# Two kinds of transposes moved from DMA to TensorE, and an in-place sum, in a fused backward kernel on one core

## The chip, the cores and the metric

The kernel runs on one NeuronCore of a Trainium2 chip. The core has a matrix engine (TensorE; PE in the profile, with its weight loads as PEld), a vector engine (VectorE, DVE), a scalar engine (ScalarE, ACT), a small general engine (GpSimd, POOL), a queue engine that here only issues DMAs (SyncE, SP), and sixteen DMA engines that all queues share. The metric is the time of one launch on the device in microseconds.

## The reference

A forward pass and its gradient are computed in one launch. In short:

```
xn  = layernorm(x)                               # 2048 x 512
K   = Re sum_n C * exp(dt*A*l) * dt*B            # 512 kernels of length 2048, 128 states each
s   = causal_conv(xn, K) + xn * Dskip            # through FFTs
f   = silu(xn @ w1) @ w2                         # 512 -> 1792 -> 512
out = x + s * silu(f)
gradients of sum(out * grad_out) for x, A, B, C (re, im), log_dt, Dskip, w1, w2
```

All inputs and outputs are bf16.

## The kernel before

The rows are held as 128 partitions x 16 tiles x 512 columns. The state-space part works by blocks b of 128 channels (4 of them), each in two halves h. The program is a set of generators, each with a letter; `play` walks through the string PLAN and lets the generator of each letter issue its next few instructions. So PLAN is an order written out by hand or by a planner, and it fixes the order of the instructions in each engine's own queue. WAYS says for each letter which of its evacuations of PSUM go to ScalarE (A) and which to DVE (D), SLOTS which buffer each tile takes. PLAN has seven parts:

- 0: loads, layer norm (6), tables (4, 5), masks (3), first rows of the forward network.
- 1: phases and powers of the state-space kernel (P, Q), its rows (R), the forward conv (X, C), the forward network (F: `gen_ffn_fwd`).
- 2: the gate (G), ds = grad_out * gate (H), transposed weights (W), forward transform of ds (D).
- 3: the backward conv (B: `gen_conv_bwd`, which leaves the gradient du in `k.ds`), dA through the network (A: `gen_da`), dx (x: `gen_dx`), the first output (O).
- 4 and 5: the gradients of A, B, C and dt. For each block, N (`gen_ssm_fold`) folds dK into G; for each of 16 groups of eight channel rows, Y (`gen_ssm_loads`) loads a transposed tile YT of the powers from DRAM, V (`gen_ssm_v`) multiplies YT with Gb into ps_v and evacuates it to Vb, T (`gen_ssm_products`) makes four products and two sums Tp, and S (`gen_ssm_sums`) sums Tp over the 21 exponents on TensorE into psS, which ScalarE copies to Sa. Z (`gen_ssm_grads`) makes the gradients of a block and stores them (gout). In part 5 also dW2 (h loads an activation block h_in, t makes a_tok = silu of it with tokens on the partitions, w multiplies) and dW1 (g loads dh_tok by DMA transposes, v multiplies).
- 6: the rest of dW1 and dW2 and the layer norm's backward: i (`gen_ln_loads`) loads pd_l (the stored dx) and Gt (grad_out), k (`gen_ln_sums`) adds du and makes two sums a row, m (`gen_ln_rows`) makes and stores the rows.

The places that the change touches:

- `gen_dw2_loads` and `gen_dw2_turns`: of 14 blocks the first nine come by a plain DMA, are turned by 16 TensorE transposes into PSUM and go through silu from there (L1197); the last five come by a DMA transpose (L1180) and go through silu in one instruction (L1194).
- `gen_ssm_loads`: every YT is two DMA transposes (L970) on SyncE's queue.
- `gen_dx`: each of 16 tiles ps_dx is evacuated to pd_s and stored to DRAM (Pd, L1171); part 6 loads it back and adds it to `k.ds` (L1270).
- `gen_ssm_fold`: ScalarE spreads G over four lanes into one tile Gf (L956); `gen_ssm_v` multiplies Gf by the masks MK into Gb (L986), both halves of Gb.
- `gen_ssm_sums`: two exponents a matmul (L1034), so psS and Sa hold two halves, which `gen_ssm_grads` adds (L1059).
- `gen_kernel_rows`: block 3's eight loads of Kb (L675) alternate between SyncE's and GpSimd's queues.

Tile pools are stacked: the last stage's pool `lw` takes the memory of `sb`, the pool of parts 4 and 5, so its first tiles wait for the last users of what lay there.

Of the kernel before, what the change touches and what calls it, by code (L numbers as in the profile page):

```python
# [10 lines left out]
ACT = mybir.ActivationFunctionType  # L11
ALU = mybir.AluOpType
# [6 lines left out]
P = 128  # L19
# [8 lines left out]
122p13273555417652067776357p577511777p747701636770773677J0J767p5787777367F66766767077F78676777633FF736746687F46F8F7486FF  # L28
F8F6666FF6F688FF56F64FJ8/XFXQFJFFFXXXPJXPXFXPFFFPXPXFPFPFQJFFFQQF9QQQFFFXFQFJQQXXQPFQXRPFFRXPXRRXFXPPFRFXPJFRRXFRPXFRQQQ
RPXQFQRQFXFRQQFFRFUFFXFQXFFFFRQRXRPRFRQXRRJPRRUPFPXRRURFRPRURQRXRFJRQCRPQFXXXXFFRQXXXQFQFQQXPQRPPFCRCCCFFFRCRCQRPCRQFRFC  # L30
RFFRFFPQRQCUQFRCFFFFCQQRFFCCQQCFCQFCXRCQQCFQCRPXFFCRXCFXCFXFPXCRPFXFCXRFCXRFJCFRRCXRPCXCFRFFQQCFRFCQQFCFRQPFFCRQPRRFCPQC
QFXFRQQRPQRCXRRRCXXJPRXRRXCUPXPRXXRCRFCPCCRQQPFFCFCFFCCPQCQFFQCRRQQCQRRXFQFCXFRFFCFQFCFCFCCCCPQJRRXCXRCCFCFFXPRRCXFPCRXC
CFCXQQCQFFQJRXPQFRCCQXCCCRQFRFQFCPRQCQRRRRRQRRRXRFPCFXRPFRFCXRCXPFURRRCXCFFRRXCCFFQFQJQQCXFXCFFCCRQCFFRCCRQQCQRFQCFRCRRR
RRCCCCXRQCCCCRCJRCRCRURRFCRRFCRCCRFFCCCCRC/CGCFCCGCCGFGFFFCCFCGCCGFGCCFGGCFCFFCGCGFCCGFCFWGCGGGGCGCFCHFCFGCGHFCCFCFCCGCH
FCGCWWCFCCCGGCWCWCCCWWHCCWCDHWHHGCCWDGMCCCWHCWWDWWDWDWLDGDWWDWWWWLWDMDDDMDDDLDDMLLWM/DEWDadDodDEDdDsBDADAAAoBDaDADdaAAAo
AsDBAoBABDWDWABADBBAasBoAAAoBBBAAAAlOBBADOaABoAADlOBBBsBxBoBDoBBDBBDEABABxDOABABxOABBBBAsxBODBoxDBxdOOBloDBoDOBxBaxDBBBD
ODEOxOBoDxBsdABBOxAOoBBBBBaAADdBDoBBaBsBBBABBBoOADAdDDAAADBAAlBoBDAAEAOooBaADBBBAddADBDABAlDBOADDADBDBAxADsoBDEOBlOAxBDO
DBAoBxxDBOABADBAABDBBADAOoABxsxDBOBoOBABAoxOABBBoOBBBADOOoDBAOoxoaBDaxDBADAdDxoBBDADBEDxOsDBBBABxAABxBOBdAOOAoBABABBBOsx
aABOBBxBsaEABxBxAABxBAABBABaBOABBdBBBxBBBaBABBBAABABBBAABABBBdBAxBsBBBsB/YNxYdYxNANNAdANAAAAxYVVAAVAVVAVaVAAxVxAVYsATAAY
NVATVxTVVAVATAVxVTVAAxsxTAVSxTAYASAVVVVAAxATAVVAVYxVTATYTTTVTxTTVxTVxVxVNTxVVSNNS/NVTVSVhTVTVVVSYTgVVtVTVhTtSSVttTVTwYTT  # L40
VTwttNhTVtgVwVSVZVVYVVthZZwtVVTNTVtTwTYZtNtwTVVTYNwZtSShvVYwtSwNVVTVVZTVTTZVVYTZtVTtVVvgVTVwTZVTZVTTtVTZSVvSVVVvSSvVVYtV
VNVVvTTvZTTVTthTZYwvVVgYtVVZZVSSTTvTVZZtwtNNwYVNthNwtTTvTVVTwVVTSVZYSVTVTwTVwVTVVvTVTTSVVYSVthVTTVZTYZTvTgStVTgZtSVVZvtv
VTVTTYVVZYVvZVhvZwSZVgtTVZtwgTvVwVVgTTgTTZvSVtwvtVvVSZVVTSTVZTVvVVZZTVwVTTTSThTwZTtSvTZZTvtSZtvwSvtZtZwvZwZvZZvZhZvwvZvZ
ZvZ/vikkgviktvwkkikigwmkhvvgvwmvigkkmvvkmvkmvihvvvwtkvmkvmvvkmikkhkvmwmkvmikwkmwvvvkwmkmvktkvvvtkmmwvkvmkwkvwkmkmkmkwwmv
wvwmmvmv
# [4 lines left out]
fp.XT=01010101;pf.pf=012012012010212120120102102102102102102102102102020210210210102102102021021021020210210210210210202  # L50
102102102102102120120210210210210210210210102102012010120120121021021021021021021021021012212012012102102012010210210210
210210202102102;fp.hT=0101010101010101;fp.ob=0101010;dft.w8=21031230132102302103210302310321;pc.pc=010101010101110101010
101010101010101010101011010101010101010101010101010101010101010101010010110101010101010101010101010110101010101010101010
101010101010101010101010101010101010101010101010101010101010101010110101010101011010101010101010101010101010101010101;tb
l.tv=01011101010110100010110100011010;tbl.ts=01010101110111010101001000101010;tbl.W=01010101010010100101;dft.t4=01001010
1010;gate.g=30124567;gate.S=01;da.doT=01010101;dftb.w8b=1010;da.dhT8=01201201;go.go_s=01010101;da.dhT6=10101010;go.go_r=
010101;go.go_g=01010101;da.pd_s=0101010101010101;go.go_x=01201201;sb.YT=0101010101010101;sb.Eb=10101010;sb.Gb=01010101;s
b.Vb=0101010101010101;sb.Tp=1010101010101010;sb.Sa=0101;fw.h_in=01010101010101;fw.a_tok=01010101010101;fw.o11=0120120120
1201;fw.dh_tok=0120120;fw.o10=0101010;lw.pd_l=01230123;lw.Gt=01230123;lw.m=01010101;lw.o1=12301230
# [100 lines left out]
def setup_tiles(k, wp):  # L160
# [28 lines left out]
    new("m4", [4])  # L189
# [22 lines left out]
def gen_plain_consts(k, w):  # L212
# [7 lines left out]
    G.memset(k.pi[:], PI_LO)  # L220
# [66 lines left out]
def gen_step_tables(k, w):  # L287
# [6 lines left out]
    pt, ph, pe, sh, kf, kk, maskf, kq, sf, sv, pj, pa, m4, rl = (  # L294
        getattr(w, nm) for nm in "p_t p_h p_e sh kf kk maskf kq sf sv pj pa m4 rl".split())
# [32 lines left out]
    TT(out=m4[:], in0=pa[:], in1=w.ia[:], op=ALU.is_equal)  # L328
    TT(out=rl[:], in0=k.ecst[:, 0:NE], in1=pj[:].to_broadcast([P, NE]), op=ALU.add)
    yield  # L330
    nc.vector.tensor_copy(out=k.MK[:, 0], in_=m4[:].unsqueeze(1).to_broadcast([P, NE, 4]))
    TT(out=k.MK[:, 1], in0=rl[:].unsqueeze(2).to_broadcast([P, NE, 4]), in1=m4[:].unsqueeze(1).to_broadcast([P, NE, 4]), op=ALU.mult)
# [290 lines left out]
def gen_kernel_rows(k, b):  # L623
# [277 lines left out]
def gen_conv_bwd(k):  # L901
# [3 lines left out]
    for b in range(4):  # L905
# [23 lines left out]
def gen_ssm_fold(k, b, sb):  # L929
# [17 lines left out]
    Gf = sb.tile([P, 32, NE, 4], BF16, name="Gf", tag="Gf")  # L947
    k.Gf[b] = Gf
# [6 lines left out]
    for bank, n in ((0, 16), (1, 5)):  # L955
        nc.scalar.copy(out=Gf[:, :, 16 * bank:16 * bank + n, :],  # L956
                       in_=G21[:, bank, 0:32 * n].rearrange("p (e q) -> p q e", e=n).unsqueeze(3).to_broadcast([P, 32, n, 4]))
        yield
# [486 lines left out]
```

## Time and profile before

| | |
|---|---|
| median of 3 runs (lowest, highest) | 576.56 us (576.12, 577.17) |
| the profiled execution | 581.0 us |
| its span, first to last instruction | 578.5 us |
| mean granted TensorE clock | 0.981 |
| PE, DVE, ACT busy | 520.2, 518.0, 451.3 us |
| HBM read, written | 58.72, 59.90 MB |

The page gives for each engine the time it was busy; the slices cut the span in forty parts and give the busy share in tenths. The view of waits lists, for each engine and line, what ended its idle time. A number of a queue (SPq, POOLq) is time in which DMAs were being issued. The window view sums busy time in a stretch. The rows of groups by line give busy us, mean ns of one, and the idle time just before them.

### The profile page before, as it was taken

Reading aid. Unit: us, or ns where it says so; the run is one execution under the profiler, and the core shown is the slowest. Engines: PE = TensorE matmul, PEld = TensorE weight load, DVE = VectorE, ACT = ScalarE, POOL = GpSimd, SP = SyncE. Lnnn points to the kernel's source line nnn. Section 1 sums busy time; section 2 is a strip of 40 time slices with the busy share of each in tenths; the row PEclk is TensorE's granted clock in tenths of the full one; section 3 lists DMA queues with packets and bytes.
Section 4 is the critical chain, followed back from the end, with each engine's and each line's share of the span. In section 5 each row is a group of like instructions: output and inputs, shape, how many; then the busy total and the mean of one; then the engine's idle time right before and its main releaser. Section 6 shows DMA issues by size and latency. Waiting matters only on the chain. (4 is left out here: it accounts for less than half of the span.)

```text
span 578.5 us, 13917 instructions
## 1 busy us (share of the span) xinstructions
PE 520.2 (90%) x5681; PEld 385.6 (67%) x5704; DVE 518.0 (90%) x814; ACT 451.3 (78%) x560; POOL 78.3 (14%) x168
## 2 busy tenths in 40 slices
PE   1497999998998989999999999999799979999983
PEld 1365768676777766876677766777567858776752
DVE  8989999999999768999999889778899989983984
ACT  7999999999998749999899866754578766643553
POOL 4321101011102030000000000000002202123221
PEclk9889999999999999999999999999899999999998
DMA  8977798988898996788779899979999999999991
GB/s 242 330 300 229 233 231 310 302 226 252 329 263 250 342 295 268 239 270 247 255 261 300 245 307 287 238 180 244 234 231 234 214 208 213 230 222 245 215 284 74
DMA packets 174032, 145.75 MB, mean 252 GB/s; under 512 B 102224, under 2 KB 151632, under 8 KB 170896
## 3 DMA queue, kind: packets, MB, share of 16 engines
q1 hardware_dynamic: 164656, 122.05, 79.0%
q0 software_dynamic: 6768, 19.93, 9.6%
q10 hardware_dynamic: 2544, 2.88, 1.5%
q8 instruction: 44, 0.72, 0.5%
q14 instruction: 20, 0.16, 0.1%
HBM read 58.72 MB, written 59.90 MB: 205 GB/s over the span
## 5 line engine op out<-in xcount | busy, mean ns | idle before, releaser
L112 ACT CAST dA<-ps_s 128x1024 bf16<-128x1024 f32 x84 | 84.4, 1034 | 7.5 <-PE ps_s L399 4.8
L755 PE MATMUL ps_h<-XT,W 128*128 128x256 bf16 x448 | 61.4, 288 | 11.4 <-ACT hT L112 8.2
L112 ACT CAST Vb<-ps_v 128x672 bf16<-128x672 f32 x59 | 41.5, 730 | 27.5 <-PE ps_v L996 17.0
L755 PEld LDWEIGHTS <-W 128*128 128x128 bf16 x448 | 44.5, 103 | 20.8 <-issue 12.9
L1146 PE MATMUL ps_da<-doT,W 128*128 128x256 bf16 x448 | 56.8, 273 | 0.0
L1235 PE MATMUL ps_w<-dh_tok,xn 128*128 128x256 bf16 x448 | 52.4, 273 | 3.7 <-ACT o L112 1.9
L1206 PE MATMUL ps_w<-YD,a_tok 128*128 128x512 bf16 x211 | 48.9, 379 | 3.7 <-ACT a_tok L1194 2.7
L1166 PE MATMUL ps_dx<-W,dhT 128*128 128x512 bf16 x224 | 51.0, 379 | 0.0
L1235 PEld LDWEIGHTS <-xn 128*128 128x128 bf16 x448 | 43.1, 98 | 10.7 <-issue 2.9
L772 PE MATMUL ps_o<-W,aT 128*128 128x512 bf16 x214 | 49.0, 379 | 1.4 <-ACT aT L763 0.5
L112 ACT CAST dB<-ps_i 128x1024 bf16<-128x1024 f32 x41 | 41.2, 1030 | 9.7 <-PE ps_i L444 8.9
L1146 PEld LDWEIGHTS <-W 128*128 128x128 bf16 x448 | 41.3, 98 | 8.5 <-issue 2.1
L1149 DVE TENSOR_TENSOR dhT<-ps_da,dhT 128x512 bf16<-128x512 f32 x56 | 37.5, 684 | 6.8 <-PE ps_da L1146 6.4
L1206 PEld LDWEIGHTS <-a_tok 128*128 128x128 bf16 x224 | 21.3, 98 | 27.0 <-ACT a_tok L1194 3.3
L772 PEld LDWEIGHTS <-aT 128*128 128x128 bf16 x224 | 21.2, 98 | 26.6 <-issue 1.6
L1166 PEld LDWEIGHTS <-dhT 128*128 128x128 bf16 x224 | 21.3, 98 | 23.4 <-issue 0.4
L996 PE MATMUL ps_v<-Gb,YT 128*128 128x168 bf16 x256 | 28.0, 242 | 3.9 <-DMA YT<-Yd 2.0
L1012 DVE TENSOR_TENSOR Tp<-Vb,Eb 128x1344 bf16<-128x1344 bf16 x32 | 27.3, 854 | 4.5 <-ACT Vb L112 3.7
L399 PEld LDWEIGHTS <-TF 128*128 128x128 bf16 x384 | 25.0, 101 | 8.5 <-issue 5.2
L574 ACT ACTIVATE sn<-V 128x2048 bf16<-128x2048 int16 (+1 forms) x16 | 30.2, 1885 | 0.3
L470 DVE TENSOR_TENSOR cm<-sp_in,dA 128x2048 bf16<-128x2048 bf16 x24 | 29.3, 1221 | 0.9
L472 DVE TENSOR_TENSOR sp_in<-sp_in,dA 128x2048 bf16<-128x2048 bf16 x24 | 29.3, 1221 | 0.6
(232 smaller groups left out, 1214.7 us busy)
## 6 DMA issues: line engine op xcount, KB each, us to landing
Yd<-YD SPq DMA_DIRECT2D x8, 1024.0 KB, 5.1
sp_in<-Ud SPq DMA_DIRECT2D x8, 1024.0 KB, 6.2
Ed<-ds SPq DMA_DIRECT2D x8, 672.0 KB, 4.0
Eb<-Ed SPq DMA_DIRECT2D x8, 672.0 KB, 6.2
h_in<-Hd SPq DMA_DIRECT2D x9, 512.0 KB, 5.2
Hd<-hT POOLq DMA_DIRECT2D x8, 512.0 KB, 4.8
Ud<-dA SPq DMA_DIRECT2D x8, 512.0 KB, 7.3
KXd<-dA SPq DMA_DIRECT2D x4, 1024.0 KB, 5.4
```

Source lines behind the costliest of these rows:

```text
L112: return self.nc.scalar.copy(out=out, in_=in_)
L470: TT(out=t2[:], in0=b[:, :, gs], in1=a[:, 1:2, gs].to_broadcast([P, 2, n, P]), op=ALU.mult)
L472: TT(out=b[:, :, gs], in0=b[:, :, gs], in1=a[:, 0:1, gs].to_broadcast([P, 2, n, P]), op=ALU.mult)
L574: nc.scalar.activation(out=sn[:, 0:n], in_=low, func=ACT.Sin, scale=-2 * PI_LO / 2.0 ** PB)
L755: nc.tensor.matmul(out=ps[:, j], lhsT=k.W1[:, dk, ft * P:ft * P + P], rhs=XTv[:, :, dk, :], start=(dk == 0), stop=(dk == DK - 1))
L772: nc.tensor.matmul(out=ps[:], lhsT=aT[:, ft, t * P:t * P + P], rhs=k.W2[:, ft, :], start=(ft == 0), stop=(ft == FT - 1))
L996: nc.tensor.matmul(out=ps[:, u, 168 * c:168 * c + 168], lhsT=YT[:, c, q + u, :], rhs=Gb[:, q0 + q + u].rearrange("p w x -> p (w x)"), star ...
L1146: nc.tensor.matmul(out=ps[:, j], lhsT=k.W2[:, ft, dk * P:dk * P + P], rhs=dTv[:, :, dk, :], start=(dk == 0), stop=(dk == DK - 1))
L1149: nc.vector.tensor_tensor(out=dh[:, i0:i0 + 2, :], in0=ps[:], in1=dh[:, i0:i0 + 2, :], op=ALU.mult)
L1166: nc.tensor.matmul(out=ps[:], lhsT=dhs[ft // 8][:, ft % 8, t * P:t * P + P], rhs=k.W1[:, :, ft * P:ft * P + P], start=(ft == 0), stop=(ft ...
L1206: nc.tensor.matmul(out=ps[:], lhsT=at[:, t, :], rhs=k.do[:, t, :], start=(t == 0), stop=(t == k.T - 1))
L1235: nc.tensor.matmul(out=ps[:], lhsT=k.xn[:, t, dk * P:dk * P + P], rhs=dh[:, t].rearrange("p j n -> p (j n)"), start=(t == 0), stop=(t == k ...
```

## The change

- All 14 activation blocks h_in come by plain DMA and are turned on TensorE, with silu from PSUM.
- Every fourth group of Y (i % 4 == 3) comes by two plain loads into a tile Yn with one buffer, and is turned on TensorE into a PSUM tile of the pool `pc`, then evacuated (new letter places of Y in PLAN and WAYS).
- The last four tiles of dx (c >= 6) are added by DVE from PSUM into `k.ds` in place, with the row sum taken on the way into a small tile `k.mx`; their stores to Pd, loads back and later additions go. The order must have them after the conv's last du.
- The fold writes its masked lanes by ScalarE with a scale per partition (`k.M4`), four instructions in place of one, straight into the first half of Gb; DVE multiplies only the second half. Gb is two buffers of a whole block; Gf is gone.
- The sums take one exponent a matmul, 21 in place of 11; Sa is half as large, and the addition of its halves is gone. Tq is half as large, and the products of a group stand in another order.
- Block 3's Kb loads of GpSimd's queue go to ScalarE's.
- A few small tiles go (`pi`, `m4`, `ddt`, which now lies in `acc`).
- PLAN, WAYS and SLOTS are new: every engine's order changes from the first part on.

```diff
-        (nc.sync, nc.gpsimd)[i % 2 if b == 3 else 0].dma_start(k.Kb[b][...], ...)
+        (nc.sync, nc.scalar)[i % 2 if b == 3 else 0].dma_start(k.Kb[b][...], ...)
...
-    Gf = sb.tile([P, 32, NE, 4], BF16, name="Gf", tag="Gf")
+    Gb = sb.tile([P, 2, 32, NE, 4], BF16, name="Gb", tag="Gb", bufs=2)
...
-        nc.scalar.copy(out=Gf[:, :, 16 * bank:16 * bank + n, :],
-                       in_=G21[...].unsqueeze(3).to_broadcast([P, 32, n, 4]))
+        for a in range(4):
+            nc.scalar.activation(out=Gb[:, 0, :, 16 * bank:16 * bank + n, a], in_=G21[...],
+                                 func=ACT.Identity, scale=k.M4[:, a:a + 1])
...
+        if i % 4 == 3:
+            for c in range(2):
+                Yn = sb.tile([P, 8, P], BF16, name="Yn", tag="Yn")
+                nc.sync.dma_start(Yn[:].rearrange("p q x -> p (q x)"), k.Yd[b, h][:, (c * 16 + q0) * P:(c * 16 + q0 + 8) * P])
+                yield
+                pt = k.pc.tile([P, 8, P], BF16, name="pt_y", tag="pc")
+                for j in range(8):
+                    nc.tensor.transpose(out=pt[:, j], in_=Yn[:, j], identity=k.ident[:])
+                yield
+                k.ev(YT[:, c], pt[:])
...
-            nc.vector.tensor_tensor(out=Gb[:], in0=k.Gf[b][...], in1=k.MK[:]..., op=ALU.mult)
+            nc.vector.tensor_tensor(out=Gb[:, 1, 16 * h:16 * h + 16], in0=Gb[:, 0, 16 * h:16 * h + 16], in1=k.MK[:]..., op=ALU.mult)
...
-        for e in range(0, NE, 2):
-            n = min(2, NE - e)
-            nc.tensor.matmul(out=psS[:, 0:n]..., lhsT=k.ident[:], rhs=Tp[:, e:e + n]..., start=(e == 0), stop=(e + 2 >= NE))
+        for e in range(NE):
+            nc.tensor.matmul(out=psS[:]..., lhsT=k.ident[:], rhs=Tp[:, e]..., start=(e == 0), stop=(e == NE - 1))
...
-    TT(out=fl(S[:, 0]), in0=fl(S[:, 0]), in1=fl(S[:, 1]), op=ALU.add)
...
+            late = c >= 6
...
+            if late:
+                r, i = 2 * c + t, 2 * (c - 6) + t
+                nc.vector.scalar_tensor_tensor(out=k.ds[:, r, :], in0=ps[:], scalar=1.0, in1=k.ds[:, r, :],
+                                               op0=ALU.mult, op1=ALU.add, accum_out=k.mx[:, i, 0:1])
+                yield
+                continue
...
-        if ft >= 9:
-            k.nc.sync.dma_start_transpose(h[:], k.Hd[ft])
-        else:
-            k.nc.sync.dma_start(h[:].rearrange("p t n -> p (t n)"), k.Hd[ft])
+        k.nc.sync.dma_start(h[:].rearrange("p t n -> p (t n)"), k.Hd[ft])
...
-        if ft >= 9:
-            k.nc.scalar.activation(out=a[:], in_=h[:], func=ACT.Silu)
-            yield
-            continue
```

More of the change, by code (lines that the diff above doesn't have):

```diff
@@ L32 @@
[L32 to L36, printed above, removed]
@@ L54 @@
[L54 to L58, printed above, removed]
@@ new lines @@
+.Gb=0101;sb.Vb=0101010101010101;sb.Tp=0101010101010101;sb.Sa=0101;fw.h_in=01010101010101;fw.a_tok=01010101010101;fw.o11=
+01201201201201;fw.dh_tok=0120120;fw.o10=0101010;lw.pd_l=012301;lw.Gt=20132013;lw.m=010101;lw.o1=12031203
+""".replace("\n", "").split(";") if x)
+WAYS = """J=AAADADAA;
+F=ADDAAAAAAADAAAAAAAADAAAAAAAAAAAAAAAAAAAAAAAAADDDAAAAAAAAAAAAADADDDADDAAA;
+X=AAAAAAADAAAAAADAADAAAAAAAAAAADDD;
+U=AA;
+R=AAAAAADAAAAADAAAAAAAAAAAAAADAAAAAADADADAAAAAAAAA;
+C=DDAAAAAAAAAAAAAAAAADDDAAAAAAAAAAAAAAADAADADADAADADDADDAAAAAAADAA;
@@ L1162, in gen_dx @@
         for t in range(2):
-            pd = da.tile([P, D], BF16, name="pd_s", tag="pd_s", bufs=2)
+            late = c >= 6
+            if late and k.du_end != (3, 8):
+                raise ValueError("du is not there yet")
+            if not late:
+                pd = da.tile([P, D], BF16, name="pd_s", tag="pd_s", bufs=2)
             ps = k.pf.tile([P, D], F32, name="ps_dx", tag="pf")
```

155 lines of the change are left out of this document (83 added, 72 removed).

## The prediction

> **What bounds the kernel now.** I read the page first (busy shares, the slices), then busy time by stretch, then the waits of the stretches in which TensorE stands still, then SyncE's own timeline there.
>
> ```profile
> span 578.5 us, 13917 instructions
> PE 520.2 (90%) x5681; PEld 385.6 (67%) x5704; DVE 518.0 (90%) x814; ACT 451.3 (78%) x560; POOL 78.3 (14%) x168
> PE   1497999998998989999999999999799979999983
> DVE  8989999999999768999999889778899989983984
> DMA  8977798988898996788779899979999999999991
> ```
>
> PE and DVE are both at 90% of the span; the DMA row is full from slice 28 on.
>
> ```profile
> 210.00:215.00 5.00, 2.30 (x31) 1.95 (x29) 1.47 (x3) 1.54 (x2) 1.98 (x3) 1.00 1.03 323
> 240.00:400.00 160.00, 157.58 (x1884) 115.82 (x1883) 144.65 (x191) 126.24 (x131) 6.50 (x12) 1.00 0.90 260
> 400.00:530.00 130.00, 120.96 (x1077) 90.63 (x1085) 112.28 (x190) 82.58 (x129) 22.82 (x41) 0.99 1.05 228
> 530.00:570.00 40.00, 35.26 (x255) 24.87 (x256) 37.08 (x96) 23.03 (x35) 7.45 (x13) 1.00 0.92 211
> 410.00:420.00 10.00, 6.58 (x64) 5.75 (x62) 7.46 (x10) 5.66 (x9) 0.00 (x0) 0.83 1.08 236
> 460.00:470.00 10.00, 8.52 (x86) 5.98 (x84) 10.00 (x21) 8.77 (x12) 1.87 (x3) 1.00 1.18 219
> 470.00:480.00 10.00, 8.10 (x65) 5.74 (x67) 7.64 (x11) 3.29 (x7) 0.00 (x0) 1.00 1.02 259
> 500.00:510.00 10.00, 9.09 (x80) 6.61 (x78) 9.77 (x18) 5.14 (x11) 3.19 (x6) 1.00 1.12 227
> ```
>
> Columns: stretch, length, busy time of PE, PEld, DVE, ACT, POOL, granted clock, DMA share. From 240 us on TensorE is the line that sets the end: idle 2.4 us up to 400, 9.0 up to 530, 4.7 up to 570, together 16.2. DVE is idle 36.0 in the same stretches. DMA is full (1.05) between 400 and 530. So an edit is worth what it takes out of those 16.2 us, less what it adds to TensorE. One more place counts, 210 to 215, where PE, DVE and ACT all stand:
>
> ```profile
> PE ps_s L399 <- DMA Kb<-KE: 2.7, 1, 2.7
> ACT dA L112 <- PE ps_s L399: 3.2, 1, 3.2
> DVE dA L113 <- PE ps_s L399: 4.1, 2, 3.1
> ```
>
> **The change part by part.**
>
> Kb. Half of block 3's Kb loads go from POOL's queue, where they stood behind a store of Od, to ScalarE's, where they stand right behind the evacuation they need. All three engines wait here, so the 2.7 us of PE's wait lie on the path: -2.7 (ends -3.1 and 0). What it costs is four issues on ScalarE, idle here (busy 1.54 of 5). Next late would be POOL's addition into Kb; in the new order it stands behind two loads of Gr that wait for nothing.
>
> Transposes from DMA to TensorE. First SyncE's timeline (start, length), then the rows by source line with shortest, median and longest issue, and below each the time to landing:
>
> ```profile
> 458.77 6.39 SPq L1221 DMA_TRANSPOSE dh_tok<-DHd  x1
> 465.26 7.56 SPq L970 DMA_TRANSPOSE YT<-Yd  x4
> ...
> L1180 SPq DMA_TRANSPOSE h_in<-Hd x5: 2702/2907/6190, 510.5 to 553.7; - x5
> DMA to landing us min/median/max: 5.9/7.8/10.4
> ...
> L1182 SPq DMA_DIRECT2D h_in<-Hd x9: 370/578/936, 410.3 to 497.0; - x9
> DMA to landing us min/median/max: 4.6/5.2/6.4
> ...
> L970 SPq DMA_TRANSPOSE YT<-Yd x32: 1237/1381/3552, 362.7 to 494.1; - x32
> ```
>
> From the chain of waits (start, length) the price of eight transposes and of eleven matmuls of the sums, and from the timeline the last blocks:
>
> ```profile
> 426.53 0.45 PE pt_t L134 x8
> 428.00 1.15 PE psS L1034 x11
> ...
> 564.84 3.63 PE L1206 MATMUL ps_w<-YD,a_tok 128*128 128x512 bf16 x16 [2.50 <-ACT a_tok L1194]
> ```
>
> Five h_in blocks and eight Y pieces leave the DMA transposes: SyncE issues 5 x (2.91 - 0.58) = 11.6 us less, and eight times at most 1.4. At 458 to 473 its queue did nothing but issue five transposes, 14 us, and PE's idle 1.48 + 1.90 = 3.4 at 460 to 480 is the wait for YT behind them: I take all of it, -3.4 (ends -4.3, with the 0.9 at 500 to 510, and 0, since fourteen dh_tok transposes stay and stand in clusters of two and three). At the end the last blocks came 7.8 us after their issue and PE waited 2.5 for a_tok: -2.5, once they are turned on TensorE (end 0: the plain load is late too). The price: 80 + 64 transposes at 0.45 / 8 = 0.056 us, +8.1 on TensorE, which has no cover for it but its own idle. Sums by single exponents: 21 matmuls of 128 columns at 0.056 are 1.18 against 1.15 for eleven, 16 times: +0.4.
>
> The Trainium skill says, in "Advanced Engine Details and Errata", X-Bar Transpose (TRN2), that "TRN2 transpose DMAs are as fast as regular DMAs". By that rule the 3.4 and the 2.5 would not come back and the sum would be 578.9; the rows do not agree with it, 7.8 us to landing against 5.2 and 2.91 us to issue against 0.58.
>
> ScalarE and DVE, from the groups by line (busy us, mean ns, idle before and its releasers):
>
> ```profile
> L134 PE MATMUL pt_t<-ident,h_in 128*128 128x128 bf16 x144 | 11.2, 222 | 0.3 <-DMA h_in<-Hd 0.3
> L1034 PE MATMUL psS<-Tp,ident 128*128 128x256 bf16 (+1 forms) x176 | 21.0, 268 | 2.2 <-ACT Sa L1037 2.2
> L956 ACT CAST Gf<-G 128x2048 bf16<-128x2048 f32 (+1 forms) x8 | 10.1, 1299 | 1.9 <-PE G L953 1.9
> L986 DVE TENSOR_TENSOR Gb<-Gf,MK 128x2688 bf16<-128x2688 bf16 x8 | 12.4, 1549 | 2.1 <-ACT Gf L956 2.1
> L1059 DVE TENSOR_TENSOR Sa<-Sa 128x512 f32<-128x512 f32 x4 | 2.7, 684 | 0.8 <-ACT Sa L1037 0.8
> L1194 ACT ACTIVATE a_tok<-h_in 128x2048 bf16<-128x2048 bf16 x5 | 9.6, 1913 | 7.0 <-DMA h_in<-Hd 7.0
> L1197 ACT ACTIVATE a_tok<-pt_t 128x1024 bf16<-128x1024 bf16 x18 | 18.6, 1041 | 0.6 <-PE pt_t L134 0.5
> L1270 DVE SCALAR_TENSOR_TENSOR pd_l<-pd_l,ds 128x512 bf16<-128x512 bf16 x16 | 11.0, 686 | 6.5 <-DMA out_dram<-gout 4.9 <-DMA pd_l<-Pd 1.6
> L112 ACT CAST pd_s<-ps_dx 128x512 bf16<-128x512 f32 x14 | 8.3, 591 | 11.6 <-issue 9.6 <-PE ps_dx L1166 1.8 <-ACT dhT L1124 0.2
> L113 DVE CAST Vb<-ps_v 128x672 bf16<-128x672 f32 x5 | 4.3, 852 | 0.1
> ```
>
> Fold: 32 ScalarE instructions for eight; sixteen of 512 elements at 0.59 and sixteen of 160 at about half of that, an estimate from the same row, 14 us against 10.1 (ends 9.5 and 19). DVE's Gb halves, 12.4 to about 6.2, and the addition of the two halves of Sa goes, -2.7: DVE -8.9. This chain (G, Gf, Gb, ps_v, and psS behind Sa) is PE's 3.4 idle at 410 to 420. Its length stays near (2.6 + 1.55 before, 3.5 + 0.8 after), but two Gb tiles let the next fold start before the last one is used up: I take half, -1.7 (ends -3.4, 0). DVE's 8.9 itself counts nothing, since DVE is not the line there; it pays if DVE is.
>
> Silu from PSUM: 10 x 1.04 - 9.6 = +0.8 on ScalarE; eight evacuations of Y, four on each engine, 1.04 or less each: both in idle time. Seventeen further evacuations go to DVE in the new lists, at 0.85 some +14.5: cover is DVE's 36.0; if that is gone they cost up to 14.5 - 8.9 = 5.6.
>
> Last dx chunks: four additions (0.69 + the accumulator's read) move from the last stretch to the end of dx: DVE -2.8 where it is busy 37.1 of 40, +2.8 where 15 are idle; four stores and two loads of 256 KB go. New wait: dx's last four tiles on the conv's last du. In the order they already stood behind it. At 0 on PE's line; -2.8 if DVE sets the end.
>
> The memory under the last stage, from the timeline (in brackets the idle before and its releaser):
>
> ```profile
> 530.49 0.69 DVE L1270 SCALAR_TENSOR_TENSOR pd_l<-pd_l,ds 128x512 bf16<-128x512 bf16 x1 [4.86 <-DMA out_dram<-gout]
> ...
> 533.50 1.52 ACT L1277 ACTIVATE pd_l<-pd_l,m,rstd 128x512 bf16<-128x512 bf16 x2 [6.18 <-DMA Gt<-in_grad_out_dram]
> 535.54 3.65 PE L1235 MATMUL ps_w<-dh_tok,xn 128*128 128x256 bf16 x32 [1.68 <-ACT o L112]
> ```
>
> The first sum of the last stage waits for the stores of gout, whose memory it takes over; ScalarE stood behind it, and PE behind ScalarE. With the new tiles the first sum waits for its own load alone, and the wait for those stores falls to the fourth chunk's o1. So PE's 1.7 goes: -1.7 (0 if ScalarE is late for another reason). DVE starts this stage up to 4.9 earlier.
>
> Order anew: no row prices it; counted at 0, with 4 either way, of the order of the waits listed here.
>
> Sum: -2.7 - 3.4 - 2.5 - 1.7 - 1.7 + 8.1 + 0.4 = -3.5. The profiled execution took 581.0, its span 578.5; the median of the runs is 576.56, 4.4 below it, and I take the sum off the median: 573.0.
>
> **The rivals.**
>
> Larger gain (0.24). With DMA and DVE both relieved all but 3 of the 16.2 go: -2.7 - 13.2 + 8.5 = -7.4, 569.2, and with 4 from the order 565. For it: DMA at 1.05, SyncE's 14 us. Against: it needs every wait at once.
>
> Slower: TensorE pays and DMA gives nothing back (0.17). The other transposes still fill SyncE's queue, YT and the last blocks come no sooner, the fold's chain stays: -2.7 - 1.7 + 8.5 = +4.1, 580.7. It decides once less than 5.8 of the 16.2 is freed. For it: PE idle only 2.4 of 160 between 240 and 400, so nothing absorbs work there; fourteen dh_tok transposes stay. Against: the waits named above. The Trainium skill's rule quoted above would bring just this case.
>
> Slower: Yn holds SyncE (0.06). Yn has one buffer, so each second half's load waits until PE has turned the first, and behind it stand h_in, GE and the next YT.
>
> ```profile
> SPq L970 <- PE ps_v L996: 12.2, 4, 5.8
> ```
>
> Such a wait took 3.05 on average; if two of the four reach PE, 573.0 + 6.1 = 579.1.
>
> No difference (0.09): the freed idle just pays for the transposes, within 0.2% (1.15 us), which is about what a measurement of this kernel can tell from no change.
>
> **How the numbers follow.** Main case 0.44, 569 to 575.4 as its own range. Faster 0.44 + 0.24 = 0.68, same 0.09, slower 0.17 + 0.06 = 0.23. Range: from 564, the larger gain with its 4 from the order, to 580, short of the upper half of the slower cases: about one tenth is left out at each end.
>
> **What would show it.** Right: no PE wait for Kb near 212; PE idle from 240 to 570 falls from 16.2 to about 7 to 10 while its busy time there grows by about 8; SyncE shows no 14 us of transposes in a row while PE waits for YT; the first sum of the last stage starts without a wait for gout; no PE wait for a_tok at the end. Wrong: PE idle stays above 13, new waits on pt_y or Yn, or DVE at 98% from 400 on with PE waiting for it.

## The result, and the profile after

The changed kernel takes 598.75 us (median of 4 runs, 596.05 to 599.73), the kernel before beside it 576.87 (4 runs). The ratio is 1.0351 with a 95% interval of 1.0277 to 1.0424: 22 us slower, where 3.5 us less had been forecast and 580 was the upper end of the range. Runs more than 1.5% above the fastest of the same kernel are left out of every ratio here (in e16 three of twelve: 585.12, 585.79 and one of 1356.1 us). The execution profiled took 596.05 us, its span 594.3. Rows of the page of the changed kernel (span, busy time of each engine, TensorE and its granted clock in forty slices), and its stretches (length, busy time of PE, PEld, DVE, ACT, POOL, granted clock, DMA share, GB/s):

```profile
span 594.3 us, 14550 instructions
PE 532.4 (90%) x6008; PEld 398.5 (67%) x6008; DVE 527.8 (89%) x830; ACT 458.5 (77%) x570; POOL 75.9 (13%) x163
PE   1488989999998989999999999979697989999994
PEclk9879999999999999999999999989898999999998
```

```profile
240.00:400.00 160.00, 155.28 (x1890) 115.02 (x1888) 143.56 (x192) 126.88 (x131) 6.50 (x12) 0.99 0.88 253
400.00:530.00 130.00, 116.87 (x1224) 91.33 (x1222) 111.79 (x187) 87.63 (x132) 16.57 (x30) 0.97 0.88 204
530.00:570.00 40.00, 40.00 (x361) 30.94 (x360) 35.60 (x90) 17.82 (x30) 10.33 (x18) 1.00 0.87 226
420.00:430.00 10.00, 6.16 (x59) 5.43 (x59) 5.10 (x7) 8.41 (x14) 0.00 (x0) 0.83 0.71 153
440.00:450.00 10.00, 5.80 (x58) 3.63 (x56) 9.96 (x22) 9.91 (x14) 0.54 (x1) 1.00 1.06 232
```

TensorE is idle 4.72 us up to 400 and 13.13 up to 530, then not at all up to 570: 17.85 together, where 16.2 stood before and 7 to 10 were forecast. DMA, full before (1.05 between 400 and 530), is now at 0.88; part of that fall is the standing of TensorE, since e1 below has 1.01 in the same stretch. That the transposes did leave the DMA shows in the page's count of packets, 174032 before and 156644 after. The clock falls to 0.83 between 420 and 430, where TensorE had stood. What it stood for is in the waits (engine, line, releaser, total, times, longest), with the group of the new fold (busy us, mean ns, idle before it) below:

```profile
PE pt_y L976 <- ACT Gb L956: 6.4, 2, 4.1
PE ps_v L1010 <- ACT Gb L956: 4.0, 1, 4.0
PE ps_v L1010 <- DVE Gb L1001: 3.8, 1, 3.8
```

```profile
L956 ACT ACTIVATE Gb<-G,M 128x512 bf16<-128x512 f32 (+1 forms) x32 | 27.5, 1123 | 7.2 <-PE G L952 7.2
L1291 DVE SCALAR_TENSOR_TENSOR pd_l<-pd_l,ds 128x512 bf16<-128x512 bf16 x12 | 8.2, 685 | 0.1
```

All four waits, 14.2 us, lead to the fold on ScalarE (the DVE instruction of the third row had itself waited 5.1 us for it). The fold takes 27.5 us where the prediction had put 14 and bounded it at 19. Two of the waits sit at pt_y, a tile of the new transposes, which draws its PSUM buffer from the pool in which the fold's source lies. The second row shows one forecast that held: the sums of the last stage no longer wait for gout's stores (0.1 us idle before them, 6.5 before the change).

### The profile page after: what moved, and what is told of

It reads as the page before. It is cut to its first block, busy times and chain, and to the rows that moved or that the text cites. A ratio compares the mean times of both kernels' runs of the same rounds, so it can differ in the third digit from the quotient of the medians.

```text
span 594.3 us, 14550 instructions
## 1 busy us (share of the span) xinstructions
PE 532.4 (90%) x6008; PEld 398.5 (67%) x6008; DVE 527.8 (89%) x830; ACT 458.5 (77%) x570; POOL 75.9 (13%) x163
## 2 busy tenths in 40 slices
DMA packets 156644, 144.75 MB, mean 244 GB/s; under 512 B 83489, under 2 KB 132897, under 8 KB 153505
## 5 line engine op out<-in xcount | busy, mean ns | idle before, releaser
L113 ACT CAST dA<-ps_s 128x1024 bf16<-128x1024 f32 x81 | 80.1, 1026 | 7.0 <-PE ps_s L425 3.4
L753 PE MATMUL ps_h<-XT,W 128*128 128x256 bf16 x448 | 59.8, 286 | 10.0 <-DVE hT L114 6.3
L113 ACT CAST Vb<-ps_v 128x672 bf16<-128x672 f32 x54 | 38.4, 730 | 36.5 <-PE ps_v L1010 33.3
L770 PE MATMUL ps_o<-W,aT 128*128 128x512 bf16 x224 | 52.3, 386 | 1.6 <-ACT hT L113 1.0
L1221 PE MATMUL ps_w<-YD,a_tok 128*128 128x512 bf16 x224 | 50.7, 379 | 0.3 <-ACT a_tok L1212 0.3
L113 ACT CAST dB<-ps_i 128x1024 bf16<-128x1024 f32 x36 | 36.0, 1019 | 12.9 <-PE ps_i L442 8.4
L1212 ACT ACTIVATE a_tok<-pt_t 128x1024 bf16<-128x1024 bf16 x28 | 28.9, 1034 | 8.6 <-PE pt_t L135 8.2
L956 ACT ACTIVATE Gb<-G,M 128x512 bf16<-128x512 f32 (+1 forms) x32 | 27.5, 1123 | 7.2 <-PE G L952 7.2
L1010 PEld LDWEIGHTS <-YT 128*128 128x128 bf16 x256 | 21.3, 101 | 13.3 <-issue 11.1
```

Source lines behind the costliest of these rows:

```text
L113: return self.nc.scalar.copy(out=out, in_=in_)
L753: nc.tensor.matmul(out=ps[:, j], lhsT=k.W1[:, dk, ft * P:ft * P + P], rhs=XTv[:, :, dk, :], start=(dk == 0), stop=(dk == DK - 1))
L770: nc.tensor.matmul(out=ps[:], lhsT=aT[:, ft, t * P:t * P + P], rhs=k.W2[:, ft, :], start=(ft == 0), stop=(ft == FT - 1))
L956: nc.scalar.activation(out=Gb[:, 0, :, 16 * bank:16 * bank + n, a], in_=G21[:, bank, 0:32 * n].rearrange("p (e q) -> p q e", e=n), func=AC ...
L1010: nc.tensor.matmul(out=ps[:, u, 168 * c:168 * c + 168], lhsT=YT[:, c, q + u, :], rhs=Gb[:, :, 16 * h + q0 + q + u], start=True, stop=True)
L1221: nc.tensor.matmul(out=ps[:], lhsT=at[:, t, :], rhs=k.do[:, t, :], start=(t == 0), stop=(t == k.T - 1))
```

## The experiments

The comparisons, 4 to 12 runs each, with the kernel before beside them (medians 576.9 to 578.2). The times are medians; the entry for the last row is its ratio times 578.2.

| run | what it is | us | ratio to before (95%) |
|---|---|---|---|
| | changed kernel | 598.75 | 1.0351 (1.0277, 1.0424) |
| e1 | changed, old fold | 581.2 | 1.0061 (1.0032, 1.0091) |
| e2 | changed, Kb back on GpSimd's queue | 599.9 | 1.0380 (1.0322, 1.0438) |
| e3 | e1 and e2 together | 584.0 | 1.0105 (1.0056, 1.0154) |
| e4 | e1, YT turned by DMA | 582.2 | 1.0117 (1.0071, 1.0163) |
| e5 | e1, h_in turned by DMA | 581.65 | 1.0078 (1.0041, 1.0114) |
| e7 | changed, fold without gaps | 583.7 | 1.0138 (1.0079, 1.0197) |
| e8 | before, new fold | 595.1 | 1.0311 (1.0244, 1.0378) |
| e10 | before, Kb on ScalarE's queue | 576.8 | 0.9985 (0.9946, 1.0025) |
| e12 | e10, new order to 240 us | 581.5 | 1.0087 (1.0054, 1.0120) |
| e13 | e3, old order to 240 us | 580.2 | 1.0045 (1.0010, 1.0080) |
| e14 | e13, YT and h_in turned by DMA | 578.9 | 1.0020 (0.9986, 1.0054) |
| e15 | e13, fold without gaps for the old one | 580.8 | 1.0050 (1.0020, 1.0079) |
| e16 | before, fold without gaps | 581.0 | 1.0048 (1.0004, 1.0092) |

### Is it the fold?

e1 puts the old fold into the changed kernel (the diffs of this part are shortened):

```diff
-        for a in range(4):
-            nc.scalar.activation(out=Gb[:, 0, :, 16 * bank:16 * bank + n, a], in_=G21[...],
-                                 func=ACT.Identity, scale=k.M4[:, a:a + 1])
+        nc.scalar.copy(out=Gf[:, :, 16 * bank:16 * bank + n, :], in_=G21[...].unsqueeze(3).to_broadcast([P, 32, n, 4]))
...
-            nc.vector.tensor_tensor(out=Gb[:, 1, ...], in0=Gb[:, 0, ...], in1=k.MK[...], op=ALU.mult)
+            nc.vector.tensor_tensor(out=Gb[:], in0=k.Gf[b][...].to_broadcast([P, 16, 2, NE * 4]), in1=k.MK[...], op=ALU.mult)
```

> The changed kernel with one part undone: ScalarE folds each bank with one broadcast copy again and VectorE masks both halves, as in the kernel before; the order, the transposes on TensorE, the sums, dx and the activations stay as changed. Theory 1 (the fold: eight masked activations take 6.7 us where one copy took 2.6, and TensorE waits 13 to 14 us for them between 380 and 500 us): the time falls by 12 to 16 us, to 582 to 587, ScalarE's fold falls from 27.5 to about 10 us, and TensorE's idle time between 380 and 500 us from 17 to about 4. Theory 2 (the new order and the transposes that TensorE took over set the time, the fold lies beside them): within 3 us of the changed kernel, 595 to 601.

581.2 us, 17.5 less than the changed kernel; a little more than the 12 to 16 of theory 1. Its stretches and busy row, to be held against those above:

```profile
PE 526.8 (91%) x6008; PEld 393.7 (68%) x6008; DVE 533.0 (92%) x831; ACT 440.8 (76%) x546; POOL 75.7 (13%) x163
240.00:400.00 160.00, 158.86 (x1911) 117.06 (x1909) 149.33 (x200) 123.77 (x126) 6.50 (x12) 1.00 0.88 255
400.00:530.00 130.00, 122.59 (x1315) 94.65 (x1314) 124.13 (x209) 76.01 (x117) 18.41 (x33) 1.00 1.01 227
530.00:570.00 40.00, 40.00 (x328) 29.63 (x327) 35.90 (x90) 23.97 (x40) 11.96 (x21) 1.00 0.78 211
```

TensorE's idle time from 240 to 570 is 1.14 + 7.41 = 8.55 us, 9.3 less. Its busy time over the whole span is 5.6 us less too (526.8 against 532.4), for the same 6008 instructions: in the changed kernel part of them ran at a lower clock (mean granted clock 0.977 against 0.988). 4.0 of the 5.6 lie in the tiles of the stretch around the fold: psS 1.8, ps_v 1.4, pt_y and pt_t 0.4 each. 9.3 + 5.6 is 14.9 of the 15.4 between the two spans. One such place in the changed kernel's timeline (start, length, in brackets the idle before), first on ScalarE, then on TensorE:

```profile
416.62 6.76 ACT L956 ACTIVATE Gb<-G,M 128x512 bf16<-128x512 f32 x8 [0.79 <-PE G L952]
```

```profile
416.71 1.33 PE L1047 MATMUL psS<-Tp,ident 128*128 128x128 bf16 x21
...
423.43 1.01 PE L976 MATMUL pt_y<-ident,Yn 128*128 128x128 bf16 x8 [4.12 <-ACT Gb L956]
424.24 2.44 PE L1047 MATMUL psS<-Tp,ident 128*128 128x128 bf16 x21
```

Eight masked copies keep ScalarE for 6.76 us, where the prediction had 3.5, and TensorE stands for 4.12 of them. The same 21 matmuls take 1.33 us ahead of the wait of 4.12 and 2.44 behind it; the granted clock is 1.00 from 416 to 418 us and 0.50 from 424 to 426. The Trainium skill, "TensorE: Matmul & The Clock Gate", Part 1: The HAM clock gate, says that the clock falls to half when TensorE has been idle for a window of about 3.4 us and comes back after as long a busy one. The trace agrees in the halving behind the wait of 4.12 us; but e3 below shows it behind waits of 1.63 and 2.04 us too, which are shorter than that window.

e8 asks the same from the other side: the new fold in the kernel before, in its own order.

```diff
-        nc.scalar.copy(out=Gf[:, :, 16 * bank:16 * bank + n, :], in_=G21[...].unsqueeze(3).to_broadcast([P, 32, n, 4]))
+        for a in range(4):
+            nc.scalar.activation(out=Gb[:, 0, :, 16 * bank:16 * bank + n, a], in_=G21[...],
+                                 func=ACT.Identity, scale=k.M4[:, a:a + 1])
```

> The kernel before, in its own order, with the masked fold of the change, and what it takes to fit into SBUF: the products with a half as large Tq and the sums by single exponents. Theory 1 (the fold costs TensorE a wait at each of the four blocks whatever the order): 577 goes to 588 to 596, with TensorE's waits behind the fold of 10 us and more. Theory 2 (only the new order brings the fold onto the path): 575 to 580.

595.1 us, 3.1% over before. The fold costs the same in either order (17.5 us over the kernel before run beside it), and its waits come up at other tiles (waits of TensorE in this kernel between 380 and 500 us):

```profile
PE psS L1033 <- ACT Sa L1036: 7.7, 2, 5.2
PE ps_v L996 <- DVE Gb L987: 3.1, 2, 2.7
```

### Why does the fold cost 27.5 us?

> This kernel leaves out all of the reference's work and writes zeros: one matmul fills a PSUM bank, and then the fold's instruction on 512 elements of each partition (128x512, F32 in PSUM to BF16 in SBUF) stands alone in eight forms, four of each, one factor changed at a time. f_as_is: as the changed kernel has it (the bank read turned, every fourth element written, the mask as scale). f_const: a constant as scale. f_copy: the same as a copy. f_packed: written without gaps. f_straight: the bank read in order, written with gaps. f_both: read in order and written without gaps. v_as_is and v_packed: on VectorE. f_wide: one copy of 2048 elements with the source broadcast, as the kernel before has it. Theory A (the writes with gaps set the 1.28 us of pitch that the changed kernel shows for 512 elements): f_packed and f_both fall to 0.45 to 0.65, f_straight stays near 1.28. Theory B (the turned read sets it): f_straight and f_both fall, f_packed stays. Theory C (the scale out of a tile sets it): f_const and f_copy fall to 0.6, all others stay. Theory D (waits inside the changed kernel and not the instruction): f_as_is itself takes about 0.6.

Seven rows of this kernel by group, four instructions each (busy us, mean ns). The four overlap a little, so from start to start one takes a quarter of the busy time, 1.2 or 0.6 us on ScalarE:

```profile
L43 ACT ACTIVATE f_straight<-G,sc 128x512 bf16<-128x512 f32 x4 | 4.8, 1420 | 0.0
L43 ACT ACTIVATE f_as_is<-G,sc 128x512 bf16<-128x512 f32 x4 | 4.8, 1389 | 0.0
L45 ACT CAST f_copy<-G 128x512 bf16<-128x512 f32 x4 | 4.8, 1388 | 0.0
L43 ACT ACTIVATE f_both<-G,sc 128x512 bf16<-128x512 f32 x4 | 2.4, 720 | 0.0
L43 ACT ACTIVATE f_packed<-G,sc 128x512 bf16<-128x512 f32 x4 | 2.4, 687 | 0.0
L46 DVE TENSOR_SCALAR v_as_is<-G,sc 128x512 bf16<-128x512 f32 x4 | 4.7, 1337 | 22.1 <-ACT f_both L43 22.1
L46 DVE TENSOR_SCALAR v_packed<-G,sc 128x512 bf16<-128x512 f32 x4 | 2.7, 734 | 0.0
```

Theory A holds: only the gaps in what is written matter. With every fourth BF16 element written, 512 elements take 1389 ns, without gaps 687; the turned read of PSUM and the scale out of a tile cost nothing (720 read in order, 1388 for a plain copy), and VectorE pays nearly the same factor (1337 against 734). The Trainium skill, "SBUF — State Buffer", Door 1: The DMA port swizzle, says that a stride is free up to "8 bf16". The stride here is 4, and the measurement disagrees for writes.

e7 takes the gaps out of the changed kernel: the four lanes lie one behind the other, and the copy of ps_v puts them back in their places.

```diff
-    Gb = sb.tile([P, 2, 32, NE, 4], BF16, name="Gb", tag="Gb", bufs=2)
+    Gb = sb.tile([P, 2, 4, 32, NE], BF16, name="Gb", tag="Gb", bufs=2)
...
-            nc.scalar.activation(out=Gb[:, 0, :, 16 * bank:16 * bank + n, a], ...
+            nc.scalar.activation(out=Gb[:, 0, a, :, 16 * bank:16 * bank + n], ...
...
-            k.ev(Vb[:, q:q + 2].rearrange("p q c w x -> p q (c w x)"), ps[:, :, 0:336])
+            k.ev(Vb[:, q:q + 2].rearrange("p q c w (e a) -> p q (c w) e a", a=4),
+                 ps[:, :, 0:336].rearrange("p q (z a e) -> p q z e a", a=4, e=NE))
```

> The changed kernel with the fold's half written without gaps: the four masked copies of a bank lie one behind the other (a outside, e inside) instead of interleaved, and the copy of ps_v to SBUF puts e and a back in their places; the number of instructions and the order stay. From the fold alone on the chip 512 elements then take 0.6 us instead of 1.2. Theory 1 (the writes with gaps are what the fold costs on the path): ScalarE's fold falls from 27.5 to about 15 us, and the time from 598.8 to 580 to 586; if the copies of ps_v don't get dearer, near the old fold's 581.2 or a little below, since VectorE has half the mask to do. Theory 2 (four instructions instead of one hold the chain, whatever each takes): 592 to 599. Theory 3 (the turned read makes the copies of ps_v dearer, 54 at 0.73 us on ScalarE): over 586 with Vb at over 0.9 us.

583.7 us: 15 come back. The groups of this kernel:

```profile
L956 ACT ACTIVATE Gb<-G,M 128x512 bf16<-128x512 f32 (+1 forms) x32 | 14.8, 600 | 7.1 <-PE G L952 7.1
L113 ACT CAST Vb<-ps_v 128x672 bf16<-128x672 f32 x54 | 38.2, 728 | 35.9 <-PE ps_v L1010 21.7 <-DVE YT L114 12.3 <-ACT Sa L1050 0.9
```

The fold is at 14.8 us, almost the 14 that the prediction had taken, and the copies of ps_v are no dearer (0.73 us). So the price was right for a fold that writes without gaps. But the kernel is still 1.4% slower than before, and 2.5 us slower than e1 with the old fold.

e16 is e8 with the same edit.

> The kernel before in its own order with the masked fold written without gaps (and the products and sums by single exponents that it needs to fit into SBUF), beside the same kernel with gaps at 595.1 us. Theory 1 (the gaps are all that the fold costs): 576 to 580. Theory 2 (four instructions for one still hold the chain by 4.8 us of ScalarE's time): 581 to 585. Less than 576 would mean that the half of the mask that VectorE is spared is worth something.

1.0048 (1.0004, 1.0092), against 1.0311 with gaps: 0.2 to 5.3 us over before, where it was 14 to 22. So the gaps are most of the fold's price there too. The time lies in theory 2's range (581.0 by the ratio; the median of the nine runs counted is 583.0), so that four instructions for one still hold the chain by a few us is not excluded. The half of the mask that VectorE is spared brings no gain that shows.

### Kb

e2 puts the Kb loads back on GpSimd's queue in the changed kernel, e3 in e1, and e10 makes the change's edit alone in the kernel before (this diff; e2 and e3 undo it):

```diff
-        (nc.sync, nc.gpsimd)[i % 2 if b == 3 else 0].dma_start(k.Kb[b][16 * i:16 * i + 16]...
+        (nc.sync, nc.scalar)[i % 2 if b == 3 else 0].dma_start(k.Kb[b][16 * i:16 * i + 16]...
```

> The changed kernel with the two Kb loads of the last block that had gone to ScalarE's queue back on GpSimd's. Theory 1 (ScalarE is held 4.96 us while it issues them, and the sums behind it move by 4 us): dB, S_b and the first da products come earlier, but the wait for Kb itself comes back, which was 5 us before the change: the time within 1.5 us of the changed kernel, 597 to 600. Theory 2 (the hold on ScalarE costs its full 4 us and Kb isn't late in the new order): 594 to 595. Theory 3 (as the prediction took it, the move is worth 2.7 us): 601.

> Both of the other two edits at once: the old fold and the Kb loads back on GpSimd's queue. If the two lie at different places of the path, the changes add: the old fold's gain plus or minus what the Kb loads alone do, 579 to 590. If the time of the old fold alone comes back to 583 and this one with it, the Kb loads are hidden either way.

> The kernel before with one part of the change: half of the last block's Kb loads on ScalarE's queue instead of GpSimd's. Theory 1 (as the prediction took it: the wait for Kb goes and nothing comes in its place): 2.7 us less than before, 573.5 to 575. Theory 2 (ScalarE is held 4 to 5 us by the issues, and dB and S_b behind them come as late as Kb did): within 1 us of before.

e10's ratio is 0.9985. Its interval, 0.9946 to 1.0025, holds 1 (theory 2), but just reaches the 0.9953 that theory 1's 2.7 us would give, so these times alone don't settle it. The changed kernel's timeline of ScalarE shows what came in the place of the wait (ACTq is time in which it issues DMAs):

```profile
209.79 4.96 ACTq L673 DMA_DIRECT2D Kb<-KE  x2
214.80 1.01 ACT L113 CAST dB<-ps_i 128x1024 bf16<-128x1024 f32 x1 [4.07 <-DMA Kb<-KE]
```

Two issues held ScalarE for 4.96 us, and the next dB waited 4.07; in e10 the same two took 2.54 us and dB waited 2.12. So theory 2's hold is seen in both.

All three comparisons lean to the side of the move, by 0.8 us (e10 against before), 1.2 (e2, inside the two intervals) and 2.8 (e3 against e1; each of e3's four runs lies above nine of e1's ten). Kb's own place doesn't explain the 2.8: from the start of the last ps_s products ahead of Kb's to the first that read Kb it takes 17.7 us in e1 and 15.9 in e3, so there the move costs 1.8 in the changed order. In the profiles the two stand 1.2 us apart at the first ps_da (251.4 and 252.6) and 5.2 at the first pt_g (442.6 and 447.8). In between e3 shows two stretches at half clock that e1 lacks (e3's timeline):

```profile
415.22 0.62 PE L976 MATMUL pt_y<-ident,Yn 128*128 128x128 bf16 x8 [1.63 <-DMA Yn<-Yd]
415.67 2.21 PE L1048 MATMUL psS<-Tp,ident 128*128 128x128 bf16 x21
...
439.46 0.45 PE L1011 MATMUL ps_v<-Gb,YT 128*128 128x168 bf16 x4 [2.04 <-ACT Gf L956]
439.75 2.38 PE L1048 MATMUL psS<-Tp,ident 128*128 128x128 bf16 x21
```

That is read from one profile of each; why the clock fell there in e3 and not in e1, which also waited 2.01 us for Gf, stays open.

e9 is the kernel before once more.

> The kernel before, unchanged, profiled once more. The profile that the prediction stands on took 581.0 us, 4.4 above the median of its runs; the gains were read from its waits and taken off the median. Theory 1 (some of those waits are that execution's own): an execution near the median lacks one or more of the halved clocks near 215 and 415 us and has shorter waits for Kb, a_tok or dh_tok. Theory 2 (they belong to the kernel): the same waits with the same lengths to 0.5 us, and the time between 576 and 582 comes from the start or from the clock alone.

577.1 us, near the median. Its longest waits of TensorE between 196 and 250 us, first, and its first ps_da products (shortest, median, longest ns; first and last start):

```profile
PE ps_s L427 <- DVE dB L113: 0.9, 2, 0.5
PE ps_s L399 <- DVE hT L113: 0.8, 1, 0.8
```

```profile
L1146 PE MATMUL ps_da<-doT,W x448: 270/273/283, 248.1 to 400.5; 128*128 128x256 bf16 x150
```

The wait of 2.7 us for Kb is not there (earlier, TensorE waited 1.9 us once for the addition into Kb), and ps_da starts at 248.1 where it started at 250.8 in the profile that the prediction used. e13 below, with Kb on GpSimd's queue and the order of before, lacks the wait too. So the 2.7 belonged to that execution.

The stretch from 460 to 480 us, where the prediction took 3.4 us, is also another. First the waits of that stretch in the prediction's profile (its timeline), then four of TensorE's waits in e9, over its whole span:

```profile
470.73 1.92 PE L1235 MATMUL ps_w<-dh_tok,xn 128*128 128x256 bf16 x16 [1.76 <-DMA dh_tok<-DHd]
473.85 0.68 PE L996 MATMUL ps_v<-Gb,YT 128*128 128x168 bf16 x7 [1.12 <-DMA YT<-Yd]
```

```profile
PE psS L1034 <- ACT Sa L1037: 2.2, 1, 2.2
PE ps_w L1206 <- ACT a_tok L1194: 2.2, 1, 2.2
PE ps_v L996 <- DMA YT<-Yd: 1.1, 1, 1.1
PE ps_w L1235 <- DMA dh_tok<-DHd: 0.3, 1, 0.3
```

Only 1.1 of the 3.4 was a wait for YT; 1.8 was for dh_tok, whose transposes stay on DMA. In e9 TensorE is idle for 0.45 us between 460 and 480 (in e10 for 0.53), though SyncE issues the same five transposes there in 13.4 us; its 1.1 for YT comes at 498 us. The waits for a_tok (2.2) and Sa (2.2) were there again; e10 has the one for Sa, but none for a_tok. This is theory 1 for Kb and dh_tok, theory 2 for Sa, and for a_tok theory 2 with e10 against it.

### The order anew, and what is left

e12 is the kernel before with Kb on ScalarE's queue and with the change's order, buffers and evacuating engines in the first three parts of PLAN; e13 is e3 with those of before. The edits are in the strings PLAN, WAYS and SLOTS alone; for PLAN, in short:

```diff
-PLAN = before[0:3] + before[3:]
+PLAN = after[0:3] + before[3:]
```

> The kernel before with Kb on ScalarE's queue and with the change's order, buffers and evacuating engines for the first three stages (to about 240 us); from the fourth stage on everything is as before. Theory 1 (the new order costs TensorE 4 to 5 us in the first 200 us, and the Kb move hides it): 4 us more than the same kernel without the new order, 577 to 582. Theory 2 (the new order is as good there): within 1 us of Kb alone, and what is left of the loss lies behind 240 us.

> The changed kernel with the old fold and Kb on GpSimd's queue (584.0 us), with the order, buffers and evacuating engines of before for the first three stages; from the fourth stage on as changed. Theory 1 (the order of the first 240 us costs 4 us): 579 to 581. Theory 2 (the loss lies behind 240 us: TensorE's transposes against the waits that they take away): 583 to 585.

The new order, with its buffers and evacuating engines, costs 4.7 us (e12 581.5 against e10 576.8), and the old one gives 3.8 back (e13 580.2 against e3 584.0): theory 1 both times. The first products ps_k, in e10 and then in e12:

```profile
L643 PE MATMUL ps_k<-W,YD x512: 197/201/212, 56.6 to 196.4; 128*128 128x84 bf16 x171
```

```profile
L643 PE MATMUL ps_k<-W,YD x512: 197/201/213, 60.6 to 201.2; 128*128 128x84 bf16 x171
```

They start 4.0 us later and end 4.8 later, so what is lost in the first 60 us is not won back there. The lines ahead of it on ScalarE, in e10 and in e12 (the sine of the step tables, and the first sine of the phases):

```profile
6.01 0.40 ACT L314 ACTIVATE sf<-kf,mpi 128x128 f32<-128x128 int32 x1
...
43.01 1.94 ACT L574 ACTIVATE sn<-V 128x2048 bf16<-128x2048 int16 x1
```

```profile
28.82 0.40 ACT L314 ACTIVATE sf<-kf,mpi 128x128 f32<-128x128 int32 x1
...
45.36 1.94 ACT L574 ACTIVATE sn<-V 128x2048 bf16<-128x2048 int16 x1
```

2.4 of the 4.0 us are there at the first sine of the phases. The step tables moved behind the magnitudes, and what is made from them now stands on VectorE just ahead of the phases. That this move is the one that delays them is read from the order; it wasn't tried alone.

e4, e5 and e14 turn on the transposes. e4 and e5 are e1 with one kind back on DMA, e14 is e13 with both (in e5 and e14 the silu of each of the last five blocks is two instructions, in the kernel before one):

```diff
-                Yn = sb.tile([P, 8, P], BF16, name="Yn", tag="Yn")
-                nc.sync.dma_start(Yn[...], k.Yd[b, h][...])
...
-                    nc.tensor.transpose(out=pt[:, j], in_=Yn[:, j], identity=k.ident[:])
+                nc.sync.dma_start_transpose(YT[:, c], k.Yd[b, h][...])
...
-        k.nc.sync.dma_start(h[...], k.Hd[ft])
+        (k.nc.sync.dma_start_transpose if ft >= 9 else k.nc.sync.dma_start)(h[...], k.Hd[ft])
```

> The changed kernel with the old fold (581.2 us) and, besides, every fourth YT turned by two DMAs on SyncE's queue again, as the others are; the order written out stays, the steps that TensorE's 64 transposes and their copies had are left empty. Theory 1 (TensorE is busy without a gap after 500 us and pays for each transpose, 64 at 0.056 us, and the DMAs would be in time): 3 to 4 us less, 577 to 578.5. Theory 2 (SyncE's transposes come late and TensorE waits for YT, as the prediction's 3.4 us had it): 580 to 583.

> The changed kernel with the old fold (581.2 us) and, besides, h_in of the last five ft turned by DMA on SyncE's queue again, so that TensorE loses 80 transposes of 0.056 us; order as changed, the steps left empty. Theory 1 (TensorE pays 4.4 us and nothing is given back): 576.5 to 578. Theory 2 (the transposes on SyncE take 2.9 us of issue each and hold YT or dh_tok behind them, which TensorE then waits for): 580 to 585.

> The kernel of the old fold with the old order of the first 240 us (580.2 us), and all 144 added transposes taken off TensorE again: every fourth YT and the last five h_in are turned by DMA on SyncE's queue as before. What is left of the change is the order behind 240 us, the sums by single exponents and the last dx chunks in place. Theory 1 (the 2.6 us that are left over before are the transposes, 8.0 us of TensorE's time that the shorter waits pay back only in part): 575 to 578. Theory 2 (the DMAs' waits come back as with each half alone, where nothing was gained): 579.5 to 582.

e4 and e5 are within 1 us of e1: theory 2, each half gives back about what it takes. e14 lies 1.3 us under e13, and its interval holds 1.0; its 578.9 falls between the ranges of the two theories. The busy rows of the whole spans (575.6 and 575.2 us), in e13 and in e14:

```profile
PE 527.5 (92%) x6008; PEld 393.2 (68%) x6008; DVE 531.5 (92%) x834; ACT 442.3 (77%) x545; POOL 78.4 (14%) x167
```

```profile
PE 520.0 (90%) x5841; PEld 385.9 (67%) x5864; DVE 529.4 (92%) x830; ACT 438.8 (76%) x541; POOL 78.1 (14%) x167
```

With the transposes TensorE is busy for 7.5 us more and idle for 7.1 less (48.1 against 55.2). Up to 2 us of both may come from the 23 matmuls that e14's trace lacks against its weight loads, an estimate from the 0.089 us that one takes in the mean (520.0 / 5841). Between 240 and 570 us DMA falls from 0.96 to 0.90, and nothing is won.

e15 puts the fold without gaps beside the old early order.

> The changed kernel with both corrections, the fold written without gaps and the old order of the first 240 us (Kb on GpSimd's queue); all else as changed. Theory 1 (fold and early order are the whole of the loss, and the rest of the change is worth what the prediction took, 3 to 4 us less its Kb term): 575 to 577. Theory 2 (the rest of the change costs 2 to 3 us as it did beside the old fold): 579 to 582.

580.8: theory 2. No kernel here is faster than before by more than its interval.

## Why the prediction was wrong, by its own steps

- **Fold, −1.7. This step failed.** Its price was taken from the evacuation of ps_dx, which writes 512 elements in one unbroken stretch (the 0.59 us), while the new instructions write every fourth element. Measured: 27.5 us against 14 taken and 19 as the upper end, 6.76 us of the chain against 3.5, 17.5 us on the kernel instead of −1.7. Without gaps it was 14.8. It was a term whose place on the path was known (the chain was named as TensorE's idle at 410 to 420) and whose price had no row with the same access pattern; no rival had a slower fold in it. The gain of 1.7 had been put on a second Gb tile. It did not show even at the right price: with the fold without gaps and two such tiles, e7 is 2.5 us over e1, e15 0.6 over e13, and e16 no faster than before.
- **The clock.** Waits were counted one for one. The new ones also brought half clock behind them: about 4 of the 5.6 us of TensorE's busy time that went with the new fold.
- **Order anew, 0 with 4 either way.** It cost 3.8 and 4.7 us in the two comparisons, at the end of that bound, and at a place that the prediction didn't look at, the first 60 us.
- **Kb, −2.7.** The wait was that execution's own, which took 4.4 us more than the median, and the issues were not free in ScalarE's idle time: they hold it. What the move is worth on the whole stays open between nothing and 2.8 us; at the place where Kb is used it costs 1.8 in the changed order.
- **Transposes, +8.1 − 3.4 − 2.5 = +2.2.** The price held (7.5 us more busy on TensorE), and the sum was near: +1.3 us by the medians, not told apart from 0. But that the sum came out near is in part luck, for the 3.4 was misread: 1.1 of it was a wait for YT, the rest mostly one for dh_tok, and in e9 and e10 the stretch has no such idle. The wait for a_tok at the end did go; one for YT of 1.6 us remains in e1. The rival in which Yn holds SyncE shows in part: TensorE waits 1.2 us for Yn in e7, 1.6 in e3, 2.2 in e15, and 0.2 in the changed kernel.
- **Last stage's memory, −1.7, sums +0.4, DVE at 0.** As forecast in the profile: no wait for gout, TensorE without idle from 530 to 570 in the changed kernel and e1, 21 matmuls of the sums in 1.33 us. None of these was measured by itself; with the fold, Kb, the early order and the transposes undone, e14 comes to before's time, so together they gave nothing that can be measured.
- **The base.** The gains were read from waits in an execution of 581.0 and taken off a median of 576.56. Where the kernel varies by more than the sum, a wait has to be seen twice before it is booked. Without the 2.7 and the 3.4, which e9 lacks, the sum is not −3.5 but +2.6. The 0.2% that the prediction took as what a measurement can tell was too fine as well: the intervals here are 0.3 to 0.7% either way.

The forecast for TensorE, idle 7 to 10 us between 240 and 570, did come true once the fold was undone (8.55 in e1). Even then the time was that of the rival in which TensorE pays and DMA gives nothing back (580.7; e1 581.2). That these two agree is chance, since the rival has no term for the early order, and e1 holds its 4 us. By medians the way from the changed kernel back is: old fold −17.5 (e1), Kb on GpSimd's queue +2.8 (e3), early order −3.8 (e13), transposes −1.3 (e14), which leaves 0.7 over before.

## What to carry to other kernels

Price an instruction from a row with the same access pattern on both sides; if there is none, measure the instruction alone before it goes on a chain that TensorE waits for. Moving transposes from a full DMA queue to a full TensorE changed idle time into busy time here and no more; it pays only if the idle time that goes is longer than the work that comes. And look at two executions before a wait is counted as a gain, and at what each wait is for.

## What the runs showed of the hardware

- Writing every fourth BF16 element doubles the time on ScalarE (1389 ns against 687 for 512 elements) and on VectorE (1337 against 734). For ScalarE, reading a PSUM bank with its two inner dimensions turned costs nothing (687 turned, 720 in order).
- Behind a wait of 1.6 to 4.1 us TensorE ran at half clock for a short while (granted clock 0.50, 21 matmuls in 2.0 to 2.4 us instead of 1.33), though not behind every such wait: e1 waited 2.01 us and kept a clock of 1.00.
- Two DMA issues on ScalarE's own queue held it for 4.96 us in the changed kernel and 2.54 in e10, against 0.67 and 0.70 for the two issues before them in the changed kernel. The same four issues on GpSimd's queue took 2.13 us in e2 and e3.
